# A planned order for all engines of an attention and MLP kernel: another order, with another way to write and issue the last output tiles

## The chip, the cores and the metric

The kernel runs on one core of one Trainium2 chip, in one launch. The metric is the device time in microseconds of that launch. The work of the core is shared by TensorE (PE, with its weight loads listed as PEld), VectorE (DVE), ScalarE (ACT), GpSimd (POOL) and SyncE (SP). SP and POOL issue the DMAs here.

## The reference, cut to what matters

A linear attention with a decaying state (RWKV-5) runs over 4 batches, 8 heads, 768 positions and a head size of 48, and its output goes through an MLP with a squared ReLU, 384 to 2048 to 384 wide.

```python
for t in range(S):
    kt, vt, rt = (k[:, :, t].copy(), v[:, :, t].copy(), r[:, :, t].copy())
    cur = np.einsum('bhd,bhe->bhde', u[None] * kt, vt)
    y[:, :, t] = np.einsum('bhd,bhde->bhe', rt, state + cur)
    state = w[None, :, :, None] * state + np.einsum('bhd,bhe->bhde', kt, vt)
...
x = np.ascontiguousarray(attn_out.transpose(0, 2, 1, 3)).reshape(B * S, H * D)
h = x @ w_in
r = np.maximum(h, 0.0)
g = r * r
return (g @ w_out).astype(np.float32)
```

All inputs and the output are float32; the output is 3072 rows by 384.

## The kernel before, in words

The positions are cut into 6 chunks of 128, and a chunk of one batch is a unit; there are 24 units, and unit i is chunk i // 4 of batch i % 4. In a unit the work goes as follows, each item a step with the name that the order uses.

- `load:i:rt`, `load:i:kt`, `load:i:vt` (L278) bring in r, k and v, 192 KB each: on POOL for units 2 to 5, on SP for all others. The pools behind them are `ldr` (3 buffers), `ldk` (8) and `ldv` (4).
- `scale:i:0` and `scale:i:1` (DVE, L300) multiply r and k by powers of the decay; `cast_v` (ACT, L304) makes v bf16.
- Units 0 to 5 are transposed by PE (`turn`, L320) and copied out of PSUM by ACT (`evict_rk`, L324). Units 6 to 23 are transposed by a DMA on SP (`turn_dma`, L309).
- `rk` (DVE, L329) and `at` (PE, L337) make products of r and k. `mask` (DVE, L349, two per unit) keeps the lower triangle. `sums` (PE, L357 and L362) makes the diagonal terms and the addition to the state; `diag_v` (DVE, L371), `state_add`, `state_decay` (DVE) and `state_cast` (ACT, L391) follow. `y_mm` (PE, L400 and L406) makes the output of the attention, `evict_y` (DVE, L415) copies it out.
- `x_turn` and `evict_x` (PE L431, ACT L435, units 0 to 5) or `x_dma` (SP, L424, the others) transpose that output for the MLP.
- `mm1:i:m:s` (PE, L447) is a part of the first product: for units 0 to 7 one unit and a quarter s of the 2048 columns (12 matmuls of 128 columns), for the others two units at a time and an eighth s (6 matmuls of 256). `relu` (ACT, L455) and `square` (ACT L462 where the last figure of the step is 1, DVE L464 where it is 0) follow.
- `mm2:i:q` (PE, L471) is a quarter q of the second product of unit i: 4 matmuls of 384 columns that add up in one PSUM bank. `evict_o` (ACT, L478) copies the bank to an `osb` tile (4 buffers), and `store` (L505) writes it to the output, by POOL or by SP as the step says.
- The last unit, 23, is done in two parts: `mm2_half:23:0` has 256 columns and `mm2_half:23:1` has 128 (PE, L486, 16 matmuls each), `evict_half` copies the first by ACT (L495) and the second by DVE (L497), and `store_half` (SP, L501) writes each.

At the start, `columns` (POOL, L241 and L242) loads w and u in another layout into the tile `wu`, `spread_log` (PE, L249) and `power` (ACT, L253) make the powers of the decay, `spread_columns` (PE, L258) and `copy_columns` (DVE) bring w and u onto partitions, and `u_columns` and `end_columns` (POOL) go on from these. `weights:...:q:I` and `weights:...:q:O` (POOL, L288 and L291) load a quarter of each MLP matrix, 384 KB in bf16, cast from float32 on the way. `fill` (PE, L245) is a matmul on constants whose result nobody reads; there are 68, all in the first part of the kernel.

No scheduler sets the order. `SCHEDULE` is one text with a word for each step; the kernel goes through the words and calls the function of that name, and each engine, POOL's and SP's DMA queues among them, does its instructions in the order in which they are written. The text behind an @ gives the PSUM banks that a step takes, of 8. Buffers rotate in the order in which they are asked for.

Of the kernel before, what the change touches and what calls it, by code (L numbers as in the profile page):

```python
# [17 lines left out]
load:0:kt fill@0 load:0:rt 2*fill load:1:rt 2*fill load:0:vt fill columns 2*fill spread_log@1 load:1:kt load:2:rt  # L18
load:1:vt weights:kt.0:0:I fill power:0 3*fill load:2:kt power:1 scale:0:0 load:9:kt 3*fill scale:0:1 turn:0:0@2
load:3:rt load:6:kt scale:1:0 fill evict_rk:0:0 fill turn:0:1@3 load:2:vt fill evict_rk:0:1 spread_columns@4  # L20
load:3:kt cast_v:0 rk:0 fill scale:2:0 at:0@5,6 copy_columns fill u_columns mask:0:1 turn:1:0@7 mask:0:0
evict_rk:1:0 weights:-:1:I sums:0@1 weights:-:2:I y_mm:0@2 diag_v:0 load:8:kt fill scale:1:1 2*fill load:3:vt fill
evict_y:0 3*fill scale:2:1 turn:1:1@3 weights:-:0:O 3*fill x_turn:0@4 turn:2:0@6 evict_x:0 fill scale:3:0
weights:-:3:I 2*fill evict_rk:1:1 4*fill evict_rk:2:0 fill rk:1 load:4:rt fill at:1@7,5 turn:2:1@2 mask:1:1
turn:3:0@4 load:5:rt evict_rk:2:1 3*fill mask:1:0 mm1:0:1:0@3 evict_rk:3:0 end_columns rk:2 fill relu:0:1:0 fill
scale:3:1 4*fill cast_v:2 fill load:6:rt at:2@6,5 cast_v:1 fill mask:2:1 4*fill turn:3:1@2 mask:2:0 sums:2@4
evict_rk:3:1 fill sums:1@7 load:4:kt diag_v:2 y_mm:1@3 y_mm:2@5 diag_v:1 mm1:0:1:1@6 weights:-:1:O evict_y:1 fill
relu:0:1:1 3*fill evict_y:2 load:4:vt 2*fill x_turn:1@2 state_add:1 evict_x:1 mm1:0:1:2@3 weights:-:2:O state_add:0
fill relu:0:1:2 fill mm1:1:1:0@6 cast_v:3 rk:3 x_turn:2@5 relu:1:1:0 state_add:2 at:3@2,7 evict_x:2 mm1:1:1:1@3
weights:-:3:O mask:3:1 square:0:1:0:1 sums:3@1 square:0:1:2:1 mask:3:0 mm1:2:1:0@6 load:7:kt square:1:1:0:1  # L30
square:0:1:1:0 mm2:0:0@4 state_cast:1 diag_v:3 y_mm:3@5 mm1:2:1:1@7 relu:2:1:0 evict_y:3 load:5:kt mm2:1:0@2
state_add:3 square:2:1:0:1 state_cast:0 x_turn:3@6 fill load:5:vt mm1:0:1:3@5 relu:1:1:1 mm1:2:1:2@1 scale:4:0
relu:2:1:1 mm1:2:1:3@3 evict_x:3 scale:5:0 fill relu:2:1:3 mm1:3:1:0@7 relu:2:1:2 mm1:1:1:3@6 scale:4:1
square:1:1:1:1 turn:4:0@3 relu:1:1:3 fill mm1:3:1:3@1 evict_rk:4:0 square:1:1:3:0 mm2:2:0@6 relu:3:1:0
square:2:1:1:0 relu:0:1:3 turn:4:1@3 fill square:2:1:3:0 mm1:3:1:1@7 evict_rk:4:1 relu:3:1:3 square:0:1:3:0 mm2:1:1
square:3:1:0:1 rk:4 mm2:0:1 relu:3:1:1 turn:5:0@5 square:2:1:2:1 at:4@3,1 state_cast:2 mm2:3:0@7 mask:4:0
square:3:1:1:1 mm2:0:2 mask:4:1 load:7:rt cast_v:4 mm2:2:1 evict_rk:5:0 sums:4@3 y_mm:4@1 diag_v:4 fill mm2:2:2
evict_y:4 mm2:2:3 scale:5:1 mm2:0:3 state_add:4 x_turn:4@5 load:8:rt turn:5:1@0 evict_x:4 scale:6:1 mm1:1:1:2@1
evict_rk:5:1 mm1:4:1:0@3 relu:1:1:2 rk:5 square:3:1:3:0 at:5@5,0 relu:4:1:0 mm1:4:1:1@1 scale:6:0 cast_v:5 mask:5:0
turn_dma:6 mm1:4:1:3@3 relu:4:1:1 mask:5:1 square:4:1:0:1 sums:5@5 mm2:3:1 diag_v:5 square:1:1:2:1 load:6:vt  # L40
square:4:1:1:0 evict_o:0 mm1:4:1:2@1 store:0:POOL scale:7:0 y_mm:5@0 relu:4:1:2 scale:7:1 mm2:1:2 relu:4:1:3
evict_y:5 turn_dma:7 mm2:1:3 state_cast:3 state_decay:4 square:4:1:3:0 x_turn:5@4 mm2:4:0@1 evict_x:5 scale:8:1
load:9:rt state_cast:4 mm2:4:1 state_add:5 load:7:vt evict_o:1 mm1:5:1:3@3 square:4:1:2:1 state_decay:5 load:10:rt
rk:6 mm1:5:1:0@0 relu:5:1:3 scale:9:1 cast_v:6 at:6@4,5 mm1:5:1:1@2 mask:6:1 mm2:4:2 scale:8:0 relu:5:1:1 rk:7
relu:5:1:0 turn_dma:8 mm2:4:3 mask:6:0 state_cast:5 sums:6@3 square:5:1:3:0 mm1:5:1:2@5 square:5:1:1:1 load:8:vt
diag_v:6 y_mm:6@2 relu:5:1:2 mm1:3:1:2@0 evict_y:6 square:5:1:0:1 at:7@4,5 square:5:1:2:1 x_dma:6 mm2:5:0@2 mask:7:1
relu:3:1:2 mm2:5:1 state_add:6 square:3:1:2:1 load:10:kt load:11:rt cast_v:7 mm2:5:2 scale:9:0 mask:7:0 mm2:3:2
turn_dma:9 scale:10:0 sums:7@0 y_mm:7@5 diag_v:7 mm2:5:3 cast_v:8 state_decay:6 evict_y:7 evict_o:4 at:8@3,4
state_cast:6 state_add:7 store:4:POOL mm2:3:3 x_dma:7 rk:8 mm1:6:1:0@1 store:1:POOL scale:10:1 load:9:vt mm1:6:1:1@5
relu:6:1:0 mask:8:1 load:11:kt mm1:6:1:3@0 mask:8:0 relu:6:1:1 square:6:1:0:1 sums:8@1 square:6:1:1:0 mm1:6:1:2@4  # L50
relu:6:1:3 state_add:8 mm2:6:0@5 relu:6:1:2 turn_dma:10 diag_v:8 evict_o:3 y_mm:8@3 square:6:1:2:1 mm2:6:1 evict_y:8
evict_o:5 state_decay:7 at:9@0,4 x_dma:8 rk:9 mm1:7:1:0@1 mask:9:0 mm1:7:1:1@7 square:6:1:3:0 load:10:vt cast_v:9
load:12:rt relu:7:1:0 mask:9:1 sums:9@3 evict_o:2 mm2:6:2 diag_v:9 square:7:1:0:1 store:2:POOL scale:11:0
mm1:7:1:3@2 relu:7:1:1 state_add:9 store:5:POOL y_mm:9@0 relu:7:1:3 mm1:7:1:2@1 evict_y:9 square:7:1:1:1 scale:11:1
at:10@4,6 x_dma:9 relu:7:1:2 state_decay:8 mm2:7:0@7 state_decay:9 square:7:1:2:1 rk:10 mm2:6:3 turn_dma:11
mask:10:1 mm2:7:1 evict_o:6 square:7:1:3:0 store:6:POOL mm2:7:2 cast_v:10 mask:10:0 load:12:kt state_cast:7
load:11:vt store:3:POOL mm2:7:3 scale:12:0 state_cast:8 sums:10@3 y_mm:10@2 diag_v:10 mm1:8:2:0@0 evict_y:10
mm1:8:2:1@1 x_dma:10 mm1:8:2:3@6 relu:8:2:1 state_cast:9 mm1:8:2:6@5 square:8:2:1:0 load:13:rt load:13:kt rk:11
at:11@4,2 relu:8:2:0 scale:12:1 mm1:8:2:4@1 relu:8:2:3 turn_dma:12 square:8:2:0:1 mm1:8:2:2@0 square:8:2:3:0
relu:8:2:4 mask:11:1 mm1:8:2:5@6 relu:8:2:2 load:12:vt mask:11:0 mm2:9:0@1 cast_v:11 load:14:rt square:8:2:4:1  # L60
state_add:10 mm1:8:2:7@2 square:8:2:2:1 sums:11@0 relu:8:2:6 y_mm:11@4 diag_v:11 mm2:8:0@3 relu:8:2:7 evict_y:11
relu:8:2:5 mm2:8:1 state_decay:10 x_dma:11 scale:13:1 square:8:2:5:1 mm2:9:1 scale:13:0 square:8:2:6:1 mm2:9:2
square:8:2:7:0 turn_dma:13 evict_o:7 at:12@5,2 rk:12 mm2:8:2 mask:12:0 load:13:vt cast_v:12 mm2:8:3 mask:12:1
load:14:kt mm2:9:3 load:15:rt sums:12@4 mm1:10:2:0@6 diag_v:12 load:15:kt y_mm:12@7 relu:10:2:0 mm1:10:2:1@5
evict_y:12 state_cast:10 rk:13 mm1:10:2:2@2 x_dma:12 state_add:11 relu:10:2:1 at:13@6,7 evict_o:9 square:10:2:1:0
mm1:10:2:6@5 square:10:2:0:1 scale:14:0 evict_o:8 mm1:10:2:3@0 cast_v:13 scale:14:1 store:8:POOL mm1:10:2:5@1
relu:10:2:2 state_add:12 turn_dma:14 store:7:POOL relu:10:2:3 mm1:10:2:7@3 mask:13:0 relu:10:2:6 mm1:10:2:4@2
square:10:2:2:1 mask:13:1 load:14:vt load:16:rt mm2:11:0@4 square:10:2:6:1 square:10:2:3:0 relu:10:2:5 sums:13@0
mm2:10:0@5 diag_v:13 relu:10:2:4 scale:15:0 square:10:2:5:1 y_mm:13@6 mm2:10:1 evict_y:13 square:10:2:4:1 scale:15:1
relu:10:2:7 mm2:11:1 x_dma:13 state_decay:11 mm2:10:2 square:10:2:7:0 turn_dma:15 state_decay:12 at:14@7,1 rk:14  # L70
mm2:11:2 cast_v:14 state_add:13 state_cast:12 mm2:10:3 load:16:kt mask:14:0 load:15:vt sums:14@2 state_decay:13
mm2:11:3 load:17:rt scale:16:0 mm1:12:2:0@6 load:17:kt mask:14:1 evict_o:11 state_add:14 mm1:12:2:1@3 relu:12:2:0
y_mm:14@0 square:12:2:0:1 diag_v:14 at:15@7,4 state_cast:11 evict_y:14 mm1:12:2:2@1 mask:15:1 x_dma:14 relu:12:2:1
mm1:12:2:7@6 scale:16:1 relu:12:2:2 mm1:12:2:5@2 square:12:2:1:0 cast_v:15 turn_dma:16 square:12:2:2:1 mm1:12:2:4@0
rk:15 mask:15:0 relu:12:2:5 mm1:12:2:3@4 relu:12:2:7 load:16:vt sums:15@3 load:18:rt relu:12:2:3 mm1:12:2:6@1
state_add:15 evict_o:10 mm2:13:0@2 relu:12:2:6 store:10:POOL state_decay:14 diag_v:15 relu:12:2:4 mm2:12:0@7
store:9:POOL square:12:2:3:0 square:12:2:6:1 y_mm:15@6 store:11:POOL square:12:2:5:1 evict_y:15 mm2:12:1
# [480 lines left out]
```

## Time and profile before

| | |
|---|---|
| runs | 177.22, 178.32 and 181.38 us; median 178.32 |
| the profiled execution | 177.38 us, with a span of 175.6 us from the first to the last instruction |
| mean granted TensorE clock | 0.997 |
| busy, share of the span | PE 97%, PEld 76%, DVE 74%, ACT 73%, POOL 19% |
| DMA | 28.83 MB, 164 GB/s on average |
| first matmul, end of the last | 1.19 us, 171.12 us |

The span is what the traces show; the device time has 1.8 us more. An engine's share is an average over stages that differ: the first 20 us have the loads of the weights, the middle has the attention of later chunks beside the MLP of earlier ones, and the last 15 us have the MLP of the last two units alone. Matmuls are pipelined, so the duration of a single one is longer than the distance to the next; the pace is read from the starts.

### The profile page before, as it was taken

Reading aid. Unit: us, or ns where it says so; the run is one execution under the profiler, and the core shown is the slowest. Engines: PE = TensorE matmul, PEld = TensorE weight load, DVE = VectorE, ACT = ScalarE, POOL = GpSimd, SP = SyncE. Lnnn points to the kernel's source line nnn. Section 1 sums busy time; section 2 is a strip of 40 time slices with the busy share of each in tenths; the row PEclk is TensorE's granted clock in tenths of the full one; section 3 lists DMA queues with packets and bytes.
Section 4 is the critical chain, followed back from the end, with each engine's and each line's share of the span. In section 5 each row is a group of like instructions: output and inputs, shape, how many; then the busy total and the mean of one; then the engine's idle time right before and its main releaser. Section 6 shows DMA issues by size and latency. Waiting matters only on the chain.

```text
span 175.6 us, 4843 instructions
## 1 busy us (share of the span) xinstructions
PE 169.5 (97%) x1946; PEld 134.0 (76%) x1946; DVE 130.0 (74%) x280; ACT 128.3 (73%) x266; POOL 32.6 (19%) x66
## 2 busy tenths in 40 slices
PE   7999999999999999999999999999999999999990
PEld 3668889868777788787786896886895976879770
DVE  4486897658998999878699989889777598560400
ACT  4616599976889499599396797499497894895930
POOL 8987444000100202200020003000030300000020
PEclk9999999999999999999999999999999999999998
DMA  5999999994797998799899999978999996410023
GB/s 109 197 221 183 218 221 214 232 166 95 156 181 136 235 157 215 175 193 155 168 157 223 182 139 257 197 139 165 191 221 173 204 199 115 82 52 19 0 90 134
DMA packets 93848, 28.83 MB, mean 164 GB/s; under 512 B 89681, under 2 KB 91730, under 8 KB 93826
## 3 DMA queue, kind: packets, MB, share of 16 engines
q1 hardware_dynamic: 89472, 18.88, 62.1%
q0 software_dynamic: 4352, 9.64, 23.1%
q8 instruction: 15, 0.25, 0.6%
q14 instruction: 7, 0.06, 0.1%
q10 hardware_dynamic: 2, 0.00, 0.0%
HBM read 20.45 MB, written 4.72 MB: 143 GB/s over the span
## 4 chain that ended last, share of the span: by engine, by line
PE 94%; ACT 1%; DVE 1%; issue 1%; POOL 0%; ACTq 0%
PE bank L447 37%; PE bank L471 35%; PE bank L245 5%; PE bank L337 4%; PE bank L400 3%; PE bank L362 2%; PE bank L406 2%; PE bank L320 2%; PE bank L486 2%; PE bank L357 1%; PE bank L249 1%; PE bank L431 1%; ACT L190 0%; ACT rkT L324 0%; ACT lnw L209 0%
## 5 line engine op out<-in xcount | busy, mean ns | idle before, releaser
L447 PE MATMUL bank<-xT,w_in_q 128*128 128x128 bf16 (+1 forms) x768 | 70.8, 246 | 0.0
L471 PE MATMUL bank<-w_out_q,g 128*128 128x384 bf16 x368 | 67.4, 326 | 0.0
L447 PEld LDWEIGHTS <-w_in_q 128*128 128x128 bf16 x768 | 64.1, 114 | 2.3
L455 ACT ACTIVATE gr<-bank 128x512 f32<-128x512 f32 x96 | 54.3, 599 | 15.5 <-PE bank L447 14.7
L471 PEld LDWEIGHTS <-g 128*128 128x128 bf16 x368 | 33.7, 98 | 19.4 <-ACT g L462 0.5
L462 ACT ACTIVATE g<-gr 128x512 bf16<-128x512 f32 x60 | 36.2, 636 | 0.5
L505 POOL DMA_DIRECT2D out_dram<-osb x21 | 11.4, 545 | 128.4 <-ACT osb L478 127.9
L349 DVE TENSOR_TENSOR am<-bank,smask 128x512 bf16<-128x512 f32 x48 | 31.7, 686 | 3.2 <-PE bank L337 2.9
L464 DVE TENSOR_TENSOR g<-gr 128x512 bf16<-128x512 f32 x36 | 24.4, 686 | 12.8 <-ACT gr L455 12.8
L391 ACT CAST stb<-st 64x192 bf16<-64x192 f32 x40 | 13.9, 348 | 5.7 <-DVE st L385 5.4
L371 DVE TENSOR_TENSOR dv<-vb,bank 128x384 f32<-128x384 bf16 x24 | 13.2, 552 | 6.3 <-PE bank L362 4.7
L300 DVE TENSOR_TENSOR rkw<-ldr,wpos 128x384 bf16<-128x384 f32 x24 | 13.3, 553 | 3.6 <-ACT wpos L253 2.4
L415 DVE TENSOR_TENSOR yb<-bank,dv 128x384 bf16<-128x384 f32 x24 | 13.3, 556 | 2.7 <-PE bank L406 1.7
L245 PE MATMUL bank<-warm 128*128 128x256 bf16 x68 | 14.0, 335 | 1.2 <-DVE warm L193 1.2
L304 ACT CAST vb<-ldv 128x384 bf16<-128x384 f32 x24 | 12.3, 511 | 3.8 <-DMA ldv<-in_v_dram 3.7
L478 ACT COPY osb<-bank 128x384 f32<-128x384 f32 x23 | 10.9, 477 | 4.9 <-PE bank L471 4.9
L300 DVE TENSOR_TENSOR rkw<-ldk,wneg 128x384 bf16<-128x384 f32 x24 | 13.3, 553 | 0.9 <-DMA ldk<-in_k_dram 0.7
L329 DVE TENSOR_TENSOR rk<-rkT 128x512 bf16<-128x512 bf16 x24 | 10.1, 421 | 4.2 <-ACT rkT L324 2.6
L381 DVE TENSOR_TENSOR st<-bank,st 64x192 f32<-64x192 f32 x32 | 11.3, 352 | 0.9 <-PE bank L362 0.6
L245 PEld LDWEIGHTS <-warm 128*128 128x128 bf16 x68 | 7.2, 116 | 3.9 <-issue 1.3
L337 PE MATMUL bank<-rkT 64*128 64x128 bf16 x192 | 9.7, 222 | 0.0
L337 PEld LDWEIGHTS <-rkT 64*128 64x128 bf16 x192 | 5.5, 95 | 5.2 <-issue 3.2
(61 smaller groups left out, 118.0 us busy)
## 6 DMA issues: line engine op xcount, KB each, us to landing
out_dram<-osb POOLq DMA_DIRECT2D x21, 192.0 KB, 3.7
ldk<-in_k_dram SPq DMA_DIRECT2D x20, 192.0 KB, 4.5
ldr<-in_r_dram SPq DMA_DIRECT2D x20, 192.0 KB, 4.4
ldv<-in_v_dram SPq DMA_DIRECT2D x20, 192.0 KB, 4.0
w_in_q<-in_moe_w_in_dram POOLq DMA_DIRECT2D x4, 384.0 KB, 9.9
w_out_q<-in_moe_w_out_dram POOLq DMA_DIRECT2D x4, 384.0 KB, 11.7
ldr<-in_r_dram POOLq DMA_DIRECT2D x4, 192.0 KB, 10.5
ldk<-in_k_dram POOLq DMA_DIRECT2D x4, 192.0 KB, 9.1
```

What stands on the lines that cost most here:

```text
L245: nc.tensor.matmul(out=bank("fill")[:, :WIDE], lhsT=warm[:, :128], rhs=warm, start=True, stop=True)
L300: nc.vector.tensor_tensor(t["rkw"][:, x, :, :, :D], pair(src), pair(wx), ALU.mult)
L337: nc.tensor.matmul(out=t["at"][o][:, p, :], lhsT=t["rkT"][sl, 1, p, :], rhs=t["rkT"][sl, 0, p, :], start=True, stop=True,)
L349: nc.vector.tensor_tensor(am, t["at"][o], smask.unsqueeze(1).to_broadcast([C, HP, C]), ALU.mult)
L371: nc.vector.tensor_tensor(t["dv"], t["vb"], t["d"].unsqueeze(2).to_broadcast([C, H, D]), ALU.mult)
L391: nc.scalar.copy(stb[b][sl, :, o * D : (o + 1) * D], st32[b][sl])
L415: nc.vector.tensor_tensor(t["yb"], t["y"], t["dv"].rearrange("p h d -> p (h d)"), ALU.add)
L447: nc.tensor.matmul(out=t["h", s][:, a], lhsT=turned, rhs=chunks[c]["xT"][:, n, b : b + m, :], start=(n == 0), stop=(n == NK - 1),)
L455: nc.scalar.activation(t["gr", s], t["h", s], AF.Relu)
L462: nc.scalar.activation(g, x, AF.Square)
L464: nc.vector.tensor_tensor(g, x, x, ALU.mult)
L471: nc.tensor.matmul(out=t["o"], lhsT=chunks[units[i][0]]["g"][:, f, units[i][1], :], rhs=w_out_q[f // 4][:, f % 4, :], start=(f == 0), stop ...
```

## The change

Only the text of `SCHEDULE` is changed. It holds the same 980 steps, each as often as before, in another order, and most of the PSUM banks are handed out anew. Because each engine follows the text, the order moves on all five engines and in both DMA queues. The text of the change says that all engines' order is planned anew with the landing of the last stores among its aims, and that the last output tiles are written and issued in another order.

The first steps, then the steps of the late units that the text below speaks of, and the end:

```diff
-load:0:kt fill@0 load:0:rt 2*fill load:1:rt 2*fill load:0:vt fill columns 2*fill spread_log@1 load:1:kt load:2:rt
-load:1:vt weights:kt.0:0:I fill power:0 3*fill load:2:kt power:1 scale:0:0 load:9:kt 3*fill scale:0:1 turn:0:0@2
-load:3:rt load:6:kt scale:1:0 fill evict_rk:0:0 fill turn:0:1@3 load:2:vt fill evict_rk:0:1 spread_columns@4
...
+load:0:kt fill@0 load:0:rt 2*fill load:1:rt 2*fill load:1:kt fill columns 2*fill spread_log@1 load:0:vt load:2:rt
+load:1:vt weights:kt.0:0:I fill power:0 3*fill load:2:kt power:1 scale:0:0 load:6:kt fill spread_columns@2 scale:1:0
+load:2:vt fill load:9:kt scale:0:1 2*fill copy_columns turn:0:0@3 load:3:rt fill evict_rk:0:0 turn:0:1@4 u_columns
...
```

On SP, the steps from `x_dma:18` on are in this order:

```text
before: x_dma:18 load:20:vt load:22:rt load:22:kt x_dma:19 load:21:vt turn_dma:21 load:23:rt load:22:vt turn_dma:22 x_dma:20 load:23:kt x_dma:21 load:23:vt turn_dma:23 x_dma:22 x_dma:23
after:  x_dma:18 load:20:vt load:22:kt load:21:rt x_dma:19 load:22:rt load:21:vt turn_dma:21 load:22:vt turn_dma:22 load:23:vt x_dma:20 load:23:kt load:23:rt x_dma:21 turn_dma:23 x_dma:22 x_dma:23
```

And the end:

```diff
-mm2:22:0@5 square:22:2:3:0 relu:22:2:4 mm2:21:2 relu:22:2:6 mm2:21:3 square:22:2:4:1 square:22:2:6:1 mm2:22:1
-evict_o:20 mm2:22:2 store:20:POOL mm2_half:23:0@0 store:19:POOL mm2:22:3 mm2_half:23:1@4 evict_o:22 evict_half:23:0
-evict_o:21 evict_half:23:1 store:21:SP store_half:23:0 store:22:SP store_half:23:1
+square:22:2:2:1 square:22:2:4:1 mm2:22:0@7 relu:22:2:6 mm2:22:1 square:22:2:5:1 mm2:20:3 square:22:2:6:1 mm2:22:2
+evict_o:21 evict_o:20 mm2_half:23:0@4 store:20:POOL mm2_half:23:1@3 evict_half:23:0 store_half:23:0 mm2:22:3
+store:21:SP evict_half:23:1 store_half:23:1 evict_o:22 store:22:SP
```

The loads of the weights are in the order I0 I1 I2 O0 I3 O1 O2 O3 before, and I0 I1 I2 I3 O0 O1 O2 O3 after. The stores that POOL issues change places among themselves.

## The prediction

> **What bounds the kernel now.** First the page, for which engine is never free, and the chain of work that ended last.
>
> ```profile
> PE 169.5 (97%) x1946; PEld 134.0 (76%) x1946; DVE 130.0 (74%) x280; ACT 128.3 (73%) x266; POOL 32.6 (19%) x66
> PE 94%; ACT 1%; DVE 1%; issue 1%; POOL 0%; ACTq 0%
> ```
>
> TensorE is busy for 97% of the span and makes 94% of the chain; no other engine passes 76%. Then the windows, for whether that holds in every stage (columns: us, then busy us and instructions of PE, PEld, DVE, ACT, POOL, then granted clock, DMA share, GB/s).
>
> ```profile
> 0.00:10.00 10.00, 8.55 (x44) 5.05 (x45) 5.37 (x26) 4.61 (x8) 8.72 (x24) 1.00 0.91 158
> ...
> 130.00:140.00 10.00, 10.00 (x96) 7.46 (x93) 7.04 (x14) 8.02 (x17) 1.40 (x3) 1.00 1.00 197
> ...
> 160.00:170.00 10.00, 10.00 (x82) 8.32 (x81) 1.99 (x3) 7.19 (x14) 1.08 (x2) 1.00 0.10 37
> 170.00:176.00 6.00, 1.11 (x18) 0.88 (x15) 0.29 (x1) 1.14 (x3) 0.00 (x0) 0.87 0.31 105
> ```
>
> From 10 to 170 us a window of 10 us holds 9.85 to 10.00 us of PE. What is left to gain is at the two ends. The timeline of the beginning shows that PE is busy there at half pace:
>
> ```profile
> 4.71 1.67 PE L245 MATMUL bank<-warm 128*128 128x256 bf16 x7
> ...
> 7.81 0.37 PE L258 MATMUL bank<-ident,wu 4*128 4x4 f32 x2
> ...
> 10.15 0.25 PE L357 MATMUL bank<-uwb,rk 128*128 128x8 bf16 x4 [0.35 <-POOL uwb L267]
> ...
> 14.09 1.15 PE L245 MATMUL bank<-warm 128*128 128x256 bf16 x9
> ```
>
> Seven fills from 4.71 to 6.18, where the next group begins, are 0.21 us each; the nine from 14.09 to 15.17 are 0.12 each. The granted clock is listed as 1.00 in both, so the pace, not that column, tells the cold stretch. The timeline of the end:
>
> ```profile
> 170.06 1.06 PE L486 MATMUL bank<-w_out_q,g 128*128 128x128 bf16 x16
> 170.25 0.48 ACT L478 COPY osb<-bank 128x384 f32<-128x384 f32 x1 [2.81 <-PE bank L471]
> 170.63 0.38 ACT L495 COPY osb_last<-bank 128x256 f32<-128x256 f32 x1
> 170.90 0.50 ACT L478 COPY osb<-bank 128x384 f32<-128x384 f32 x1
> 171.15 0.29 DVE L497 COPY osb_last<-bank 128x128 f32<-128x128 f32 x1 [5.87 <-PE bank L486]
> 171.42 0.37 SPq L505 DMA_DIRECT2D out_dram<-osb  x1
> 171.84 0.42 SPq L501 DMA_DIRECT2D out_dram<-osb_last  x1
> 172.31 0.44 SPq L505 DMA_DIRECT2D out_dram<-osb  x1
> 172.85 0.40 SPq L501 DMA_DIRECT2D out_dram<-osb_last  x1
> ```
>
> PE ends at 171.12. The first store on SP is that of tile 21, whose copy stands behind two others on ACT (170.25, 170.63, 170.90) though its product was done long before; so all four stores begin only at 171.42 and queue. The last is issued at 172.85 and lands 1.7 us later (DMA part), at 174.5; the span ends at 175.60, 4.48 us behind PE.
>
> **The change part by part.** Every step is in both lists the same number of times (980 words, 68 fills); functions, buffers and counts are the same. So PE's own work is the same, and the time changes only by where PE waits and by what follows its end. I compare steps by the PE work that the two lists put ahead of them, with starts from before's rows: 12 mm1 matmuls of 128 columns 0.67 us, 6 of 256 0.66, four of mm2 0.65, a warm fill 0.11, an `x_turn` 0.17.
>
> *The end, -0.84 us.* In the new list tiles 21 and 20 are copied by ACT ahead of the last half tile; PE ends with mm2_half:23:0, mm2_half:23:1 and the last quarter of tile 22. Call PE's end T. The 256-column half ends at T-1.54 (0.89 for the other half, 0.65 for the quarter), is copied 0.03+0.38 later and issued by SP from T-1.13 to T-0.7; store 21 until T-0.3; the 128-column half (copied by DVE at T-0.33) until T+0.1. Tile 22 is copied from T+0.03 to T+0.52 and issued at T+0.55 with SP free; an `osb` store on SP lands 2.0 us after its issue, T+2.55, and 1.09 us more (174.51 to 175.60) end the span at T+3.64 against T+4.48. Bounds: -0.94 if it lands after 1.9, as the other full store on SP did, and +0.86 if it takes the 3.7 that is the median on POOL. I take the SP row, since the engine and size are the same. Tile 20's store goes on POOL right after the first copies, some 3 us ahead of T; with POOL's median of 3.7 it lands by T+0.7 and hides. The reordered earlier stores on POOL cost nothing: POOL is busy 19% of the span; they are reordered among themselves only.
>
> *The beginning, +0.5 us.* Ahead of mm1:0:1:2 the new list has the same PE work as the old but for three fills and `x_turn:1`, which now come behind: 0.49 us less ahead, so 0.49 more behind. That step reads weight quarter w_in_q 2. POOL issued it at 10.8 us, and its landing took 10.6:
>
> ```profile
> L288 POOL DMA_DIRECT2D w_in_q<-in_moe_w_in_dram x1: 775/775/775, 10.8 to 10.8; - x1
> DMA to landing us min/median/max: 10.6/10.6/10.6
> ```
>
> So it lands at 21.4; before ran the step at 21.48, just behind. On POOL the same loads stand ahead of it in both lists, so it lands at the same time; the step can't start earlier, and PE's end moves by at least 21.4-21.48+0.49 = +0.4. More if PE idles more on the way there: `spread_columns` now follows five fills of that stretch in place of ten fills and the eight transposes of unit 0, so PE reaches it at 5.8 (4.71 plus 5 times 0.21), but its operand u lands 3.6 us after the issue at 3.03, at 6.6: 0.85 idle. `y_mm:0` now waits for masks behind `scale:1:1` on DVE, about 0.25. Before idles 0.6 on this way (0.35 for uwb and 0.14 and 0.10 around the 4x4 transposes). Extra idle is thus 0.5, PE comes to mm1:0:1:2 at 21.5, after the landing. I take +0.5; the bounds are +0.1 (the landing 0.3 earlier) and +1.2 (none of before's 0.6 saved).
>
> A rule bears on the same stretch. The Trainium skill, "TensorE: Matmul & The Clock Gate", Part 1: The HAM clock gate, says that PE runs at half clock until an activity window of about 3.4 us, free-running against the program, has been busy. The two paces of the fills agree. By it the change of pace can fall up to a window sooner or later from run to run, an estimate of 1.7 us of PE time; a window later would make the sum 179.3.
>
> *The middle, 0.* I looked for places where the new list leaves less PE work between a step and what it needs. The shortest from a mm1 to its mm2 falls from 2.28 to 1.72 us (mm2:8:3). Needed are relu 0.60, square 0.69 and the handovers, about 1.5. The shortest from the scores `at` to `y_mm` past the start is 1.57; the two masks take 1.29 at once. The engines that hide this are ACT and DVE at 7 to 9 us in 10, so their cover is thin: 0, bounds 0 and +1.
>
> *Around 130 to 150 us, +0.4.* SP's loads and transposes are almost without room here, and PE takes their results as they land:
>
> ```profile
> 131.14 0.71 SPq L278 DMA_DIRECT2D ldr<-in_r_dram  x1
> ...
> 138.31 2.53 SPq L309 DMA_TRANSPOSE rkT<-rkw  x1
> ...
> 145.67 0.40 PE L337 MATMUL bank<-rkT 64*128 64x128 bf16 x8
> ```
>
> The first is load:22:rt, the second turn_dma:22, which landed 7.3 us later at 145.6; at:22 ran at 145.67. The new list puts load:22:rt behind x_dma:19 (1.53 us on SP, not ready before evict_y:19): about 133.4. With its 3.9 us it lands at 137.3, and scale:22:0, whose place on DVE is about 136.5, waits 0.8 with state_add:19, evict_y:20 and rk:21 behind it. turn_dma:22 follows at about 138 and lands at 145.3 with before's 7.3. at:22 has one quarter of mm2 (0.65) less ahead, so it is wanted at 145.0 or, if the earlier half microsecond has been lost, 145.4. I take +0.4 for this and mm1:20:2:0, which has y_mm:22 (0.37) less ahead; 0 if the transposes land in 5.1 as the one before, +2 if the load is slow too.
>
> *ACT at the end, +0.15.* relu:22:2:0 is first of its group on ACT, and its mm1 now runs third: two mm1 steps ahead, one quarter less, 0.66 later. ACT needed 7.06 us from that relu (160.02) to the last square (167.08), and mm2_half:23:0 began 0.58 later. 0.66 uses this up: about 0.1 to 0.2; bounds 0 and +0.7.
>
> Sum: -0.84+0.5+0+0.4+0.15 = +0.21. The profiled execution took 177.38 (span 175.6 and 1.8 around it), so 177.6. The median of the runs shown, 178.32, is 0.9 above that execution and the three runs spread over 4 us; about 2% is what a measurement of this kernel can tell from no change.
>
> **The rivals.** *The load that came too late (slower, 0.18).* One place: scale:22:0. Between load:22:rt and it the new list leaves 3.35 us of PE work where the shortest past the start was 5.6. It decides once the load lands after 137.7. If it takes the 7.3 of the transpose beside it, it lands at 140.7, the transpose is issued at 141.3 and lands 5.1 to 7.3 later, 146.4 to 148.6; PE, wanting 145, stands 1.4 to 3.6, in place of 0.4: 178.6 to 180.8. For it: SP issues 1 to 2 us behind its place at 130. Against: the loads around it took 3.9.
>
> *The end gained and nothing lost elsewhere (0.12).* Weights land 0.3 sooner, the transposes take 5.1, ACT has room: 177.38-0.84+0.1 = 176.6. Against it is the landing at 21.4, for the same bytes stand ahead.
>
> *The end is not shortened (0.08).* The last store is now a full tile of 192 KB, where it was 64 KB that landed in 1.7. If it takes 2.9 to 3.7, it gains nothing or loses 0.86, and the costs of 1.05 stay: 178.4 to 179.3. Against: two full SP stores, 1.9 and 2.0.
>
> *The full pace comes later (0.12).* In before the fills quicken at 14.0, 3.9 us behind PE's last early pause (10.15). In the new list the last early pause is that ahead of `y_mm:0`, near 12.0; if the quick pace again comes 3.9 us behind it, that is 1.9 later, in which PE does half the work: +0.95, 178.5. For it: the pace before the two pauses was slow although PE was busy. Against: the pause ahead of `y_mm:0` is short, and may not count. A sooner pace gains nothing, since the weights hold mm1:0:1:2 at 21.4. This is the rule named above, in this kernel's rows.
>
> **How the numbers follow.** The forecast has 0.50, its own range 176.9 to 178.5. To leave no more than 2 in 10 out, the range goes down to 176.0 and up to 180.2, into the slow load. Below 174 (2%) none of the cases ends: 0.04 for what I don't see. Above 180.9 lies the far end of the slow load, above all when the late pace or a stall in the middle comes on top: 0.14. Within 2%: 0.82.
>
> **What would show it.** PE still about 97%, no group new in the waits. Right on the end: the last SP issue is a full `osb` store some 0.6 us behind PE's last matmul, and 3.6 us from PE's end to the span's. Right on the beginning: the `spread_columns` row (L258) has an idle of 0.8, and the third mm1 group starts at 21.4 or later. Right on the late part: rkw scaling waits for ldr around 137. It is wrong if PE's end moves by more than 2 us, or down.

## The result, and the profile after

| | before | after |
|---|---|---|
| median of 16 executions each | 178.31 us | 177.19 us |
| the profiled execution | 177.38 us, span 175.60 | 176.95 us, span 175.05 |
| end of the last matmul | 171.11 us | 171.57 us |
| from there to the end of the span | 4.49 us | 3.48 us |

The ratio of the times is 0.9949, with an interval of 0.9924 to 0.9973: 0.9 us faster, clear of the noise, and inside the 2% that the chances call the same. The difference of the medians is a little larger, since four of the executions of before lie at 181.4 to 182.1 us, which the ratio leaves out.

The table already holds the main reading. In the profiled executions the end gives 1.01 us, and everything ahead of it takes 0.46 back, as PE ends that much later. The busy line and the chain of the page after:

```profile
PE 167.7 (96%) x1946; PEld 132.1 (75%) x1946; DVE 128.8 (74%) x280; ACT 128.1 (73%) x266; POOL 33.2 (19%) x66
PE 76%; DMA 9%; ACT 6%; DVE 4%; SPq 2%; issue 1%; DVEq 0%
```

PE is busy for 1.8 us less with the same 1946 matmuls, as the full pace came 4.3 us sooner (table below), and yet it ends 0.46 later: what the pace saved went into waits. The chain now leaves PE in several places (DMA 9%, where it was PE 94% before). The windows (columns as in the prediction):

```profile
0.00:10.00 10.00, 8.21 (x44) 4.90 (x44) 4.99 (x25) 4.03 (x6) 9.09 (x24) 1.00 0.91 159
10.00:20.00 10.00, 8.31 (x120) 6.75 (x115) 7.83 (x16) 4.51 (x10) 8.99 (x17) 1.00 1.19 207
130.00:140.00 10.00, 10.00 (x94) 7.50 (x90) 6.93 (x15) 7.65 (x17) 0.00 (x0) 1.00 1.08 169
160.00:170.00 10.00, 10.00 (x84) 8.26 (x82) 1.99 (x3) 7.34 (x15) 0.54 (x1) 1.00 0.02 8
```

The idle time stands in the first 20 us, 3.5 us of it. From 130 to 140 us PE is full, as before. The timeline of the beginning (start, duration, engine, line, operation, and in brackets the idle time ahead of it and who ended it):

```profile
4.71 1.25 PE L245 MATMUL bank<-warm 128*128 128x256 bf16 x5
6.50 0.44 PE L258 MATMUL bank<-ident,wu 4*128 4x4 f32 x2 [0.54 <-DMA wu<-in_w_dram]
...
12.45 0.36 PE L400 MATMUL bank<-vb,am 128*128 128x48 bf16 x8 [1.37 <-ACT vb L304]
...
15.00 1.15 PE L245 MATMUL bank<-warm 128*128 128x256 bf16 x9
...
21.23 0.83 PE L447 MATMUL bank<-xT,w_in_q 128*128 128x128 bf16 x12
```

`spread_columns` waits for u, as predicted. `y_mm:0` waits for 1.37 us, and for another reason than predicted: for `vb`, the cast of v, which ACT could make only when `load:0:vt` landed at 11.87 us; on SP this load now stands behind `load:1:kt`. The nine fills from 15.00 to 15.98 are at 0.11 us each, the full pace, in spite of that pause. And the third mm1 group starts at 21.23, 0.25 sooner than before's, with 0.49 us less work ahead of it: 0.24 is lost here. PE goes into it straight from a fill at 21.12, without a wait. The weight quarter that it reads:

```profile
L288 POOL DMA_DIRECT2D w_in_q<-in_moe_w_in_dram x1: 772/772/772, 10.8 to 10.8; - x1
DMA to landing us min/median/max: 10.0/10.0/10.0
```

It was issued at the same 10.8 us as before, but landed in 10.0 us, at 20.84, where before's took 10.6 and came at 21.38.

The end of the timeline:

```profile
167.57 0.91 ACT L478 COPY osb<-bank 128x384 f32<-128x384 f32 x2
168.12 2.80 PE L486 MATMUL bank<-w_out_q,g 128*128 128x256 bf16 x32
170.07 0.37 ACT L495 COPY osb_last<-bank 128x256 f32<-128x256 f32 x1 [1.58 <-PE bank L486]
170.47 0.36 SPq L501 DMA_DIRECT2D out_dram<-osb_last  x1
170.76 0.81 PE L471 MATMUL bank<-w_out_q,g 128*128 128x384 bf16 x4
170.88 0.43 SPq L505 DMA_DIRECT2D out_dram<-osb  x1
171.41 0.40 SPq L501 DMA_DIRECT2D out_dram<-osb_last  x1
171.61 0.48 ACT L478 COPY osb<-bank 128x384 f32<-128x384 f32 x1 [1.17 <-PE bank L471]
172.12 0.33 SPq L505 DMA_DIRECT2D out_dram<-osb  x1
```

SP issues its first store at 170.47, ahead of PE's end, where before it began at 171.42, behind it. Tiles 21 and 20 are copied at 167.57, and the four stores don't queue on SP any more. The last one is issued 0.55 us behind PE's end, lands 1.84 later, and the span ends 1.09 behind that: 0.55 + 1.84 + 1.09 = 3.48.

### The profile page after: what moved, and what is told of

It is laid out like the page before. It is cut to its first block, busy times and chain, and to the rows that moved or that the text cites. A ratio compares the mean times of both kernels' runs of the same rounds, so it can differ in the third digit from the quotient of the medians.

```text
span 175.1 us, 4846 instructions
## 1 busy us (share of the span) xinstructions
PE 167.7 (96%) x1946; PEld 132.1 (75%) x1946; DVE 128.8 (74%) x280; ACT 128.1 (73%) x266; POOL 33.2 (19%) x66
## 4 chain that ended last, share of the span: by engine, by line
PE 76%; DMA 9%; ACT 6%; DVE 4%; SPq 2%; issue 1%; DVEq 0%
PE bank L447 31%; PE bank L471 30%; DMA ldv<-in_v_dram 4%; PE bank L337 4%; DMA rkT<-rkw 3%; PE bank L245 2%; PE bank L400 2%; PE bank L362 2%; ACT gr L455 2%; DMA xT<-yb 2%; SPq L278 2%; PE bank L406 2%; PE bank L486 2%; ACT g L462 1%; DVE g L464 1%; ACT osb L478 1%
## 5 line engine op out<-in xcount | busy, mean ns | idle before, releaser
L447 PE MATMUL bank<-xT,w_in_q 128*128 128x128 bf16 (+1 forms) x768 | 72.4, 246 | 0.3 <-DMA xT<-yb 0.3
L455 ACT ACTIVATE gr<-bank 128x512 f32<-128x512 f32 x96 | 53.7, 603 | 20.2 <-PE bank L447 18.9
L471 PE MATMUL bank<-w_out_q,g 128*128 128x384 bf16 x368 | 68.5, 326 | 0.0
L447 PEld LDWEIGHTS <-w_in_q 128*128 128x128 bf16 x768 | 64.1, 114 | 3.6 <-issue 0.5
L462 ACT ACTIVATE g<-gr 128x512 bf16<-128x512 f32 x60 | 37.0, 641 | 0.4
L381 DVE TENSOR_TENSOR st<-bank,st 64x192 f32<-64x192 f32 x32 | 11.2, 351 | 0.2
L324 ACT COPY rkT<-bank 128x512 bf16<-128x512 bf16 x12 | 6.9, 585 | 6.0 <-PE bank L320 5.9
L400 PE MATMUL bank<-vb,am 128*128 128x48 bf16 x192 | 8.6, 183 | 1.4 <-ACT vb L304 1.4
L400 PEld LDWEIGHTS <-am 128*128 128x128 bf16 x192 | 7.8, 96 | 2.6 <-issue 1.4
## 6 DMA issues: line engine op xcount, KB each, us to landing
w_out_q<-in_moe_w_out_dram POOLq DMA_DIRECT2D x4, 384.0 KB, 11.4
```

What stands on the lines that cost most here:

```text
L400: nc.tensor.matmul(out=y[:, 2 * p + o, :], lhsT=t[f"am{o}"][:, p, :], rhs=t["vb"][:, 2 * p + o, :], start=(o == 0 and p == 0), stop=c == 0 ...
L447: nc.tensor.matmul(out=t["h", s][:, a], lhsT=turned, rhs=chunks[c]["xT"][:, n, b : b + m, :], start=(n == 0), stop=(n == NK - 1),)
L455: nc.scalar.activation(t["gr", s], t["h", s], AF.Relu)
L462: nc.scalar.activation(g, x, AF.Square)
L471: nc.tensor.matmul(out=t["o"], lhsT=chunks[units[i][0]]["g"][:, f, units[i][1], :], rhs=w_out_q[f // 4][:, f % 4, :], start=(f == 0), stop ...
```

## The experiments

The theory, A: the whole gain is the end's, copies and stores; at the beginning PE arrives at the landing of w_in_q 2 in either order, or near it, so that neither its pace nor a pause nor the fills ahead of it count for the time. The rivals: B, that the full pace, which comes at 9.7 us in place of 14.0, makes the gain; and C, that what PE has to do ahead of the third mm1 group, the fills with it, sets the time. Later runs have rivals of their own, told in their expectations. Experiments 1 to 4 ran on one chip (before 178.16 us there), 5 to 8 on another (178.40), 9 to 12 on a third (178.08); ratios are against before on the same chip. "Third group" is the start of `mm1:0:1:2`, "tail" is from PE's last matmul to the end of the span, both in the profiled execution. In the experiments' own files the lines stand two lower (L445 for L447, and so on).

**1. Before with the new end.**

```diff
-evict_o:20 mm2:22:2 store:20:POOL mm2_half:23:0@0 store:19:POOL mm2:22:3 mm2_half:23:1@4 evict_o:22 evict_half:23:0
-evict_o:21 evict_half:23:1 store:21:SP store_half:23:0 store:22:SP store_half:23:1
+evict_o:21 evict_o:20 mm2:22:2 store:20:POOL mm2_half:23:0@0 store:19:POOL mm2_half:23:1@4 evict_half:23:0
+store_half:23:0 mm2:22:3 store:21:SP evict_half:23:1 store_half:23:1 evict_o:22 store:22:SP
```

> The old list with the new order of the last steps alone: tile 21 copied first, the two halves of unit 23 ahead of the last quarter of tile 22, and the stores in that order. Theory A (the gain is made at the end; the two beginnings come out alike because a landing of weights sets both): PE ends where it did or within 0.2 us of it, the span ends 3.5 us behind PE in place of 4.5, and the time is 0.994 of before's. Theory B (the gain is the earlier full pace of PE at the beginning, and the end is worth little): the time is 0.998 to 1.000.

Measured: 177.12 us, 0.9946 (0.9927 to 0.9966); tail 3.59. The end alone, in the old order, gives the 0.9 us of the whole change. The profiled execution is the slowest of the seven (177.75): PE's end, expected within 0.2 us of before's, came 1.27 later there. The first 0.5 of that is a wait of the third group for the weights, which landed at 21.90 that time:

```profile
21.95 0.86 PE L445 MATMUL bank<-xT,w_in_q 128*128 128x128 bf16 x12 [0.77 <-DMA w_in_q<-in_moe_w_in_dram]
```

**2. After with the old end.**

```diff
-evict_o:21 evict_o:20 mm2_half:23:0@4 store:20:POOL mm2_half:23:1@3 evict_half:23:0 store_half:23:0 mm2:22:3
-store:21:SP evict_half:23:1 store_half:23:1 evict_o:22 store:22:SP
+evict_o:20 mm2_half:23:0@4 store:20:POOL mm2:22:3 mm2_half:23:1@3 evict_o:22 evict_half:23:0 evict_o:21
+evict_half:23:1 store:21:SP store_half:23:0 store:22:SP store_half:23:1
```

> The new list with the old order of the last steps. Theory A: 1.0 us is given back, 4.5 us from PE's end to the span's, and the time is 0.999 to 1.002 of before's. Theory B: the gain stays, 0.994 to 0.996.

Measured: 178.12 us, 1.0005 (0.9987 to 1.0022); tail 4.49. The rest of the change is worth nothing, within -0.2 to +0.4 us. With experiment 1 this is the split: the end -0.9, all the rest 0.1.

**3. After without 16 of the fills** between `x_turn:0` and `turn:3:0`, 1.75 us of PE's work at the full pace.

```diff
-x_turn:0@5 mask:1:1 6*fill mask:1:0 3*fill turn:2:1@1 scale:3:0 fill weights:-:3:I evict_rk:2:1 3*fill scale:3:1
-2*fill evict_x:0 fill turn:3:0@4
+x_turn:0@5 mask:1:1 mask:1:0 turn:2:1@1 scale:3:0 weights:-:3:I evict_rk:2:1 scale:3:1 evict_x:0 turn:3:0@4
```

> The new list without 16 of the fills that stand between x_turn:0 and turn:3:0 (1.75 us of PE work at full pace). Theory A (a landing of weights sets when mm1:0:1:2 can start): PE stands idle where the fills were, that step still starts at 21 us, and the time is as that of the changed kernel, 0.993 to 0.997 of before's. Theory C (PE's work, fills included, sets the time from its first instruction on): 1.5 us faster than the changed kernel, 0.986. If the idle time brings the slow pace back: over 1.00.

Measured: 178.11 us, 0.9997 (0.9971 to 1.0022). From the timeline of PE:

```profile
16.86 0.40 PE L318 MATMUL bank<-identb,rkw 128*128 128x128 bf16 x4 [1.27 <-DVE rkw L298]
...
21.13 0.83 PE L445 MATMUL bank<-xT,w_in_q 128*128 128x128 bf16 x12
```

With 1.75 us less to do, the third group starts 0.1 sooner: the fills had covered a wait of `turn:3:0` for DVE's scaling, and the weights (landed at 20.85) would have let it start only 0.2 sooner still. That speaks against C. But the kernel also lost the 0.9 us that the end had given, and A had no place for that. In the profiled execution PE is 0.1 us ahead of after's up to 63 us; then `turn_dma:9`, issued at 58.20 (after: 58.30), lands at 64.50 where after's landed at 63.44, and PE is 0.7 behind after's at 65 us. It loses another 0.6 up to 75 us, where it waits for a transpose of the output; experiments 2 and 7, which have all their fills, lose 0.3 to 0.4 at that place too. Why these transposes land later is not settled, and so neither is whether the missing fills have to do with it: the interval begins at 0.9971, and that of after ends at 0.9973.

**4. Before without its early pause:** two of the fills behind `y_mm:0` go ahead of `sums:0`, which waited 0.35 us for `uwb`.

```diff
-evict_rk:1:0 weights:-:1:I sums:0@1 weights:-:2:I y_mm:0@2 diag_v:0 load:8:kt fill scale:1:1 2*fill load:3:vt
+evict_rk:1:0 weights:-:1:I 2*fill sums:0@1 weights:-:2:I y_mm:0@2 diag_v:0 load:8:kt scale:1:1 fill load:3:vt
```

> The old list with two of the seven fills behind y_mm:0 moved ahead of sums:0, where PE paused 0.35 us for uwb. If the quick pace comes 3 to 4 us behind PE's last pause, the fills quicken near 11 to 12 us in place of 14.0. Theory A: the time stays within 0.3% of before's, since mm1:0:1:2 still waits for its weights at 21.4. Theory B (the earlier pace is what gains): 1 to 1.5 us faster, 0.992 to 0.995.

Measured: 178.12 us, 0.9996 (0.9976 to 1.0016). The full pace came at 10.2 us in place of 14.0:

```profile
12.92 1.15 PE L243 MATMUL bank<-warm 128*128 128x256 bf16 x9
...
19.22 0.33 PE L360 MATMUL bank<-vb,rkw 128*128 128x96 bf16 x4 [0.85 <-ACT vb L302]
...
21.47 0.75 PE L445 MATMUL bank<-xT,w_in_q 128*128 128x128 bf16 x10
```

The third group starts at 21.47, before's at 21.48: PE is at 19 us sooner, waits there for the cast of v, and comes to the landing (21.4) as before. B is refuted.

**5. After with the half tile last:** the last quarter of tile 22 goes ahead of both halves, so the last store is the 64 KB piece.

```diff
-mm2:22:2 evict_o:21 evict_o:20 mm2_half:23:0@4 store:20:POOL mm2_half:23:1@3 evict_half:23:0 store_half:23:0 mm2:22:3
-store:21:SP evict_half:23:1 store_half:23:1 evict_o:22 store:22:SP
+mm2:22:2 evict_o:21 evict_o:20 mm2:22:3 store:20:POOL store:21:SP mm2_half:23:0@4 evict_o:22 store:22:SP
+mm2_half:23:1@3 evict_half:23:0 store_half:23:0 evict_half:23:1 store_half:23:1
```

> The new list with another end: the last quarter of tile 22 runs ahead of the two halves of unit 23, so that the last thing PE makes is the half of 128 columns, and the last store is its 64 KB. Theory A (what counts is how soon behind PE's end the last SP store is issued, and how long it lands): the DVE copy takes 0.29 in place of ACT's 0.49 and the store lands in 1.7 in place of 1.84; PE's end to the span's falls from 3.48 to about 3.1 us, and the time to 0.992 to 0.993 of before's (the changed kernel had 0.995). A rival: the gain comes from tile 21's copy alone, and the order of the last three steps makes no difference: 0.995.

Measured: 176.60 us, 0.9888 (0.9862 to 0.9915); tail 2.98.

```profile
169.19 2.80 PE L484 MATMUL bank<-w_out_q,g 128*128 128x256 bf16 x32
171.54 1.15 SPq L499 DMA_DIRECT2D out_dram<-osb_last  x2
172.03 0.29 DVE L495 COPY osb_last<-bank 128x128 f32<-128x128 f32 x1 [6.56 <-PE bank L484]
```

The two full stores of SP are away before PE ends (172.00), and what follows PE is a copy of 0.29 us and a small store. It takes another 0.5 us off the tail. The time fell more than the 0.992 that was expected, and the rival's 0.995 lies outside the interval, which does not reach that of experiment 6 on the same chip.

**6. After with v of unit 0 loaded ahead of k of unit 1 on SP,** as before had it; this takes away the pause of 1.37 us.

```diff
-load:1:rt 2*fill load:1:kt fill columns 2*fill spread_log@1 load:0:vt
+load:1:rt 2*fill load:0:vt fill columns 2*fill spread_log@1 load:1:kt
```

> The new list with load:0:vt back ahead of load:1:kt on SP. In the changed kernel vt0 landed at 11.87 us, cast_v:0 waited for it and PE stood 1.37 us ahead of y_mm:0. Here that pause falls under 0.4 us. Theory A (the landing of w_in_q 2 sets the third mm1 group): that group still starts at 21 us or later, and the time is that of the changed kernel within 0.2%, 0.993 to 0.997. Theory C (PE's pauses add up to the end): 1 us faster than the changed kernel, 0.989.

Measured: 177.29 us, 0.9945 (0.9920 to 0.9970), as after.

```profile
11.85 0.53 PE L398 MATMUL bank<-vb,am 128*128 128x48 bf16 x8
...
21.07 0.86 PE L445 MATMUL bank<-xT,w_in_q 128*128 128x128 bf16 x12
```

The pause is gone, the third group comes 0.16 us sooner, 0.05 behind the landing of its weights, and the time is the same. The chain of after gives "DMA ldv" 4% of the span; taking that wait away was worth nothing that was measured.

**7. After with `mm2:20:3` ahead of the last group of mm1,** as a cover for its wait, and its relu first in its group on ACT.

```diff
-mm2:20:2 mm1:22:2:3@4 ... relu:22:2:0 relu:22:2:7 ... relu:22:2:3 relu:22:2:1 ... square:22:2:5:1 mm2:20:3 square:22:2:6:1
+mm2:20:2 mm2:20:3 mm1:22:2:3@4 ... relu:22:2:3 relu:22:2:0 relu:22:2:7 ... relu:22:2:1 ... square:22:2:5:1 square:22:2:6:1
```

> The new list with mm2:20:3 moved ahead of the first mm1 of the last group, where PE waited 0.48 us for the transpose of unit 23, and relu:22:2:3 moved to the head of its group on ACT, as its mm1 is. If PE's waits behind the first 25 us go to the end one for one: 0.3 to 0.5 us faster than the changed kernel, 0.992 to 0.993. If ACT's run of relus and squares sets when the last halves start, PE waits there in its place, and the time stays at 0.995.

In after this is a wait that the prediction did not have; here it is gone. First after's row, then this kernel's:

```profile
158.98 3.44 PE L447 MATMUL bank<-xT,w_in_q 128*128 128x256 bf16 x30 [0.32 <-DMA xT<-yb]
```

```profile
159.39 3.44 PE L445 MATMUL bank<-xT,w_in_q 128*128 128x256 bf16 x30
```

Measured: 176.65 us, 0.9907 (0.9875 to 0.9939), in the medians 0.5 us less than after (0.6 less than experiment 6, on the same chip); the intervals overlap. The profiled execution doesn't end sooner than those of experiments 6 and 9 (a span of 174.85 us against 174.88 and 174.86), because PE is 0.4 to 0.5 us later than theirs at 155 us. From the mm2 group that begins there to the first half of tile 23, PE takes 12.42 us, against 12.87 in after, so the trace bears out a gain of 0.4 to 0.5 at this place.

**8. After with the landing made later:** `load:3:vt` goes ahead of `weights:-:2:I` on POOL.

```diff
-weights:-:2:I mask:0:1 fill evict_rk:1:0 fill load:7:kt fill load:3:vt
+load:3:vt weights:-:2:I mask:0:1 fill evict_rk:1:0 fill load:7:kt fill
```

> The new list with load:3:vt ahead of the weight quarter w_in_q 2 on POOL, so that this quarter lands about 1.1 us later (21.9 in place of 20.8). Theory A: mm1:0:1:2 starts at 22.0 in place of 21.2, and the time grows by 0.6 to 0.9 us, 0.998 to 1.000. Theory D (the landing has room, and the end is set elsewhere): no change, 0.995.

```profile
22.13 0.86 PE L445 MATMUL bank<-xT,w_in_q 128*128 128x128 bf16 x12 [0.95 <-DMA w_in_q<-in_moe_w_in_dram]
```

Measured: 178.02 us, 0.9970 (0.9949 to 0.9991). The weights landed at 22.08 and PE stood for 0.95 us; the median is 0.7 above experiment 6 on the same chip, where the intervals just overlap. The ratio lies between the two theories: under A's 0.998 to 1.000, and D's 0.995 is only just inside the interval. In the traces the third group starts 1.06 later than in experiment 6, and PE ends 1.26 later. It is the counterpart of experiment 6: a pause of 1.37 us ahead of the landing costs nothing that was measured, while most of a later landing comes out at the end of the kernel.

**9. After, repeated** beside the next three (no edit).

> The changed kernel once more, beside the three below on one chip: 0.994 to 0.996 of before's. PE's end to the span's about 3.5 us again; the third mm1 group starts near 21.2 wherever the fills quicken.

Measured: 177.19 us, 0.9963 (0.9944 to 0.9981); tail 3.50, third group 21.15.

**10. After with the edits of 5 and 7.**

> The new list with the end of e5 (tile 22's last quarter ahead of the halves, so that the last store is 64 KB) and the late fill of e7 (mm2:20:3 ahead of the last mm1 group, relu:22:2:3 first). If the two gains add up, 0.4 to 0.5 us each: 0.986 to 0.990 of before's. If ACT's squares set when the halves start in both, only one of them: 0.990 to 0.992.

Measured: 176.67 us, 0.9916 (0.9885 to 0.9946); span 174.30, tail 2.97. The median shows no sum of the two: it is as 5 or 7 alone. In the trace the tail is that of 5, but of the 0.45 us that 7 gained behind 155 us only 0.25 is left: the last quarter of tile 22, now ahead of the halves, waits for ACT's last square.

```profile
167.86 0.44 PEld L469 LDWEIGHTS <-g 128*128 128x128 bf16 x4 [0.40 <-ACT g L460]
```

Experiment 11 has the same wait. That is a part of what its expectation called ACT setting the start of the halves; the interval of 0.6% is too wide to see the rest in the times.

**11. The same with the edit of 6.**

> e10 with load:0:vt ahead of load:1:kt as in e6. Theory A (the weights set the third mm1 group): as e10 within 0.2%. Theory C: 1 us below e10.

Measured: 176.52 us, 0.9914 (0.9888 to 0.9940): as 10.

**12. Before with the end of experiment 5,** in place of the two lines that experiment 1 took out:

```diff
+evict_o:21 evict_o:20 mm2:22:2 store:20:POOL mm2:22:3 store:19:POOL store:21:SP mm2_half:23:0@0 evict_o:22 store:22:SP
+mm2_half:23:1@4 evict_half:23:0 store_half:23:0 evict_half:23:1 store_half:23:1
```

> The old list with the end of e5. Theory A (all that separates the two lists is the end): 1.4 us off before's, 0.991 to 0.993, as e5 with the new list. If the new list has a gain of its own beside its end: 0.994 or more.

Measured: 176.32 us, 0.9917 (0.9884 to 0.9950); tail 3.08.

```profile
168.22 2.80 PE L484 MATMUL bank<-w_out_q,g 128*128 128x256 bf16 x32
170.57 1.15 SPq L499 DMA_DIRECT2D out_dram<-osb_last  x2
171.06 0.29 DVE L495 COPY osb_last<-bank 128x128 f32<-128x128 f32 x1 [5.87 <-PE bank L484]
```

The old order with this end does as well as the new order with it (5, 10, 11): outside the last 8 us the two orders can't be told apart by their times. Experiments 5, 7, 10, 11 and 12 are all faster than before by 0.8 to 1.1%; among themselves they are not told apart.

## Why the prediction was right, and where it was not

The time, 177.19 us (176.95 profiled), lies in the range and in the forecast's own range of 176.9 to 178.5, and the change is inside 2%, as its 0.82 had it. But the point of 177.6 is 0.2 above before's profiled execution, and the kernel became faster; the sum failed in its costs. Experiment 2 puts all that is not the end at +0.1 us, against +1.05. That the point is only 0.4 off is luck: costs that were about 1 us too high were added to one execution of before that was 0.9 under its median, and the two errors cancel. In outcome this is the rival that was given 0.12, "the end gained and nothing lost elsewhere".

**The end, -0.84: right in mechanism, 0.17 too small.** The profiled executions show -1.01, experiment 1 a ratio that comes to 0.96 us. The issue 0.55 behind PE's end and the 1.09 behind the landing were as predicted; the store landed in 1.84 us and not 2.0. Before's 4.49 in place of 4.48 is rounding. The rival of a late full store (2.9 to 3.7 us) did not come.

**The beginning, +0.5: the step that failed most.** The landing of w_in_q 2 was rightly picked as what holds the third group, and experiment 8 shows it. The failure is in the sentence "so it lands at the same time", with a bound of 0.3 us: it landed 0.54 sooner in this execution. PE's arrival, put at 21.5, came at 21.23 by two errors against each other: up to 20 us PE idled 1.9 us more than before (0.5 was put down), and the sooner pace saved 1.8 (nothing was put down). So in this execution PE's arrival, 0.39 behind the landing, set the start of the group. In the executions that were profiled with the same POOL order as after (after, experiments 2, 3, 5, 6, 7, 9, 10, 11) the weights landed between 20.82 and 21.66 us, and in eight of these nine within 0.3 us of the third group's start, in six of them 0.05 ahead of it:

| | full pace from | w_in_q 2 landed | third group |
|---|---|---|---|
| before | 14.0 | 21.38 | 21.48 |
| after | 9.7 | 20.84 | 21.23 |
| 1, before with the new end | 9.5 | 21.90 | 21.95 |
| 4, before without its early pause | 10.2 | 21.4 | 21.47 |
| 12, before with the half last | 13.4 | 21.3 | 21.38 |
| 2, after with the old end | 11.2 | 21.30 | 21.35 |
| 5, after with the half last | 11.2 | 21.66 | 21.71 |
| 6, after without the pause | 12.5 | 21.02 | 21.07 |
| 7, after with a late cover | 12.7 | 20.85 | 21.07 |
| 8, weights later | 11.4 | 22.08 | 22.13 |
| 9, after again | 9.6 | 21.10 | 21.15 |

(Landings are worked out as the issue plus the time to landing.) The landing thus moves by as much from one execution to the next as the term that was computed from it. The +0.24 of the profiled execution is one draw; over the runs this term can't be told from nothing. Of the idle times, `spread_columns` was right (0.73 us from the end of its fills at 5.77, predicted 0.85), and `y_mm:0` was wrong: 1.37 us for v, where 0.25 was put down for the masks. The move of `load:1:kt` past `load:0:vt` on SP had not been counted. By experiment 6 it cost 0.16 us at the third group and nothing that was measured in the time: without it the weights hold the group, which starts 0.05 behind their landing.

**The middle, 0: right.** Neither `mm2:8:3` nor `y_mm:12` has an idle time in after. In other executions of the same steps PE waits in the middle for transposes (0.3 to 0.4 us at 73 us in experiments 2 and 7), inside the bounds of 0 to +1.

**130 to 150 us, +0.4: too much.** `load:22:rt` was issued at 132.81 (predicted 133.4) and landed 3.1 us later, at 135.89, not 3.9; the scaling ran at 135.92, so the predicted wait of 0.8 on DVE was not there. `turn_dma:22` was issued at 137.08 instead of 138, and `at:22` came without a wait; `at:21` waited for 0.2. The rival of the load that came too late did not come either.

**ACT at the end, +0.15: nothing.** The first half of tile 23 follows at 168.12 without a wait. What the step missed is the wait of 0.48 us (by the distance of PE's rows; the profile's bracket gives 0.32 of it) at 158.98 for `x_dma:23`, which experiment 7 removes.

**The full pace comes later (rival, 0.12): refuted.** It came sooner, 9.7 us, 3.2 behind the pause that ended at 6.50, and the far longer pause ahead of `y_mm:0` did not bring the slow pace back. Nor would it have counted: in experiment 7 the pace came 3.0 us later than in after, and the third group started 0.16 sooner; experiment 4 moved it by 3.8 us for a ratio of 0.9996. The Trainium skill, "TensorE: Matmul & The Clock Gate", Part 1: The HAM clock gate, has the pace follow an activity window of about 3.4 us that runs free against the program, with a ramp of under 1% of a typical span. The traces agree in part: after, 2, 5, 7 and 9 have the same instructions up to 20 us, and the pace came at 9.6 to 12.7 us, 3.1 apart. But before and experiment 1 have the same first steps too, and there it came at 14.0 and 9.5, 4.5 apart, which is more than one window; and the slow stretch, from the first matmul at 1.19, lasted 8 to 13 us and not about 3.4. What else the pace hangs on is not shown. The 1.7 us that the prediction estimated from that rule did not reach the total: by experiment 4 the stage behind begins with a landing.

**What would show it.** Of the signs that were named, the last SP issue (0.55 behind PE) and the tail (3.48 for 3.6) came, the third group started at 21.23 in place of 21.4 or later, and the wait of the scaling around 137 did not come. The idle time ahead of `spread_columns` came (0.54 in its row, 0.73 by the starts, for 0.8). PE fell to 96%, and the waits have groups that are new (`y_mm:0`, `x_turn:0`, the mm1 at 158.98), against "no group new". PE's end came 0.46 later, inside the 2 us that were named.

**Open.** Whether experiment 3's 0.9 us has to do with its missing fills, or only with transposes that landed later; what became of the rest of 7's gain in the times of 10; and what sets the moment of the full pace.

## What to carry to other kernels

The end of a kernel is a chain of its own, copy, issue, landing: copy products in the order in which they are done, let every store but the last be issued while the main engine still works, and make the last piece the smallest. In the stages ahead of it, find the landing or the handover that a stage begins with before counting work in front of it; as long as the main engine gets there by the landing, work, pace and pauses ahead of it neither cost nor gain, and a chain of waits lists them all the same. Take a landing's spread from several executions, not from one, before a term of a sum is hung on it.

## What was not expected of the hardware

The moment at which PE's pace doubles (a fill of 0.21 us becomes 0.11 to 0.12) moved between 9.6 and 12.7 us for the same instructions of after's list, and between 9.5 and 14.0 for those of before's (experiment 1 and before), while the granted clock is listed as 1.00 in this stretch. A weight quarter of 384 KB, issued at 10.8 us in before and after alike, landed 0.54 us apart in these two executions. A full store of 192 KB on SP, with little other traffic, landed in 1.84 us, hardly more than the 64 KB piece that ended before's span in 1.7.
